# Attention, gated and bilinear layers on one core: query scaling moved to GpSimd, conversion passes and loads moved in time

## The chip, the cores and the metric

The kernel runs on one core of one Trainium2 chip. The metric is the device time of one execution in microseconds; the median of three runs of the kernel before is 1085.52 us (1084.79 to 1085.8). All rows below come from one profiled execution of that kernel.

## The reference

Three layers follow one another. All inputs but q, k, v and tau come as float64.

```python
scores = (1/8) * q @ k.T                 # 4 batches, 8 heads, 576 tokens, head size 64
thresh = max(scores) - tau               # scores below it are dropped
attn   = exp(scores - max(scores)) over the kept ones, divided by its sum
x = (attn @ v)                           # laid out as 2304 tokens x 512
h = x @ w_in;  y = (h * tanh(softplus(h))) @ w_out        # 512 -> 2048 -> 512
out = ((y @ w_a) * (y @ w_b)) @ w_out2                    # 512 -> 1536 -> 512
```

## The kernel before, in words

The first quarter of the time is attention, the rest the two dense layers; the change touches attention alone. The core works on 16 pairs of heads (4 batches, 4 pairs each). A pair is five units: c = 0 to 3 are 128 query rows each for both heads, c = 4 holds the last 64 rows of both heads at once. That makes 80 units, n = 0 to 79, and the loop in `attention` (L833) has one iteration per unit, written out by hand: the order of the calls is the order on each engine, and each engine works through its own list in order.

In iteration n these happen:

- `least` (L683), VectorE: reads the scores of unit n from PSUM, multiplies them by the constant column `nsc` (minus 1/8), writes them as `s` to SBUF and accumulates their least value `m`. One instruction per head.
- `bars` (L692), GpSimd: one small addition, `te` = `m` + tau.
- `turned` (L736): TensorE turns the masked weights of unit n-2, ScalarE copies them out of PSUM (`pt`).
- `expo` (L696), ScalarE: the exponential `ex` of unit n.
- `weighted` (L755), TensorE: products with v of unit n-4, into `sums_o`; ScalarE copies them out as `u`.
- `scores` (L669), TensorE: the scores of unit n+1. PSUM has room for one unit, so they need `least` of unit n to have read it.
- `mask` (L705), VectorE: reads `s` and `ex` from SBUF, writes `pm`. It belongs to unit n-1. After the last unit of a pair `invert` (L712) does two tiny VectorE operations on `sm`, and `send` (L787) multiplies `u` by the inverse sums and writes it to DRAM as `xd`.

Between them lies other work. The float64 weights are narrowed to float32 in `narrow` (L94), one block per pair of heads, 15 blocks during attention (`ask`, L796, starts one; `convert(n, k)`, L803, runs its next stage k units after the unit `due`, which has c = 4):

- k = 0: ScalarE takes the low words (L107, "low pass") and then the high words (L109, "sign-seeing pass")
- k = 1: VectorE shifts (L111), GpSimd adds (L112)
- k = 2: ScalarE takes the sign (L119)
- k = 3: GpSimd multiplies (L123, the "conversion product"), SyncE writes the block to DRAM

Inputs come through SyncE's queue. `load_qk` asks for q and k of the next pair at c = 0, `load_v` for v at c = 4. `prepare(0, 0)` (L255) sets up the first dense layer: four loads of `xd` into tiles `b` (first calls `b<-xd`), and for each a ScalarE pass `H` (L290, `x<-b`) and a VectorE pass `L` (L294, the remainder). Its plan at n = 48 puts the loads at n = 49, 59, 64, 54 and the passes H, L, H, L, ... at n = 52, 55, 57, 60, 62, 65, 67, 70.

Of the kernel before, what the change touches and what calls it, by code (L numbers as in the profile page):

```python
# [8 lines left out]
F32 = mybir.dt.float32  # L9
F32R = mybir.dt.float32r  # L10
I32 = mybir.dt.int32
I16 = mybir.dt.int16
U32 = mybir.dt.uint32
AF = mybir.ActivationFunctionType
ALU = mybir.AluOpType
PSUM = bass.MemoryType.PSUM
# [23 lines left out]
SEEN = 0.501 / (1.125 * 2.0 ** -15)  # L40
# [3 lines left out]
def tile_attn_mish_bilinear(ctx, tc, qd, kd, vd, vd2, tau, w_in, w_out, w_a, w_b, w_out2, out):  # L44
    nc = tc.nc
    V, A, G, PE = nc.vector, nc.scalar, nc.gpsimd, nc.tensor
# [11 lines left out]
    nsc = const.tile([128, 1], F32, name="nsc")  # L58
# [35 lines left out]
    def narrow(kind, f):  # L94

        w, block, _ = SOURCES[kind]
        shape, nm = [128, CC, 128], f"{kind}{f}"
        tl = lambda s, dt, bufs: cv.tile(shape, dt, tag="cv" + s, name=s + nm, bufs=bufs)
        raw = cv.tile([128, CC, 256], U32, tag="wraw", name="raw" + nm, bufs=3)
        nc.sync.dma_start(out=raw, in_=block(w, f).bitcast(U32))  # L100
        words = raw.rearrange("p c (n t) -> p t c n", t=2)
        hi, lo = words[:, 1], words[:, 0]
        for _ in range(WAIT[len(mish_on)]):
            yield True
        early = not mish_on
        a, o = tl("a", I32, 2), tl("f", F32, 2)
        A.activation(unit[:, 0::2].rearrange("p (c n) -> p c n", c=CC), lo, AF.Copy, scale=2.0 ** -29)  # L107
        if early:
            A.activation(o.bitcast(I32), hi.bitcast(F32), AF.Copy, scale=SEEN)  # L109
            yield True  # L110
        V.tensor_scalar(out=a, in0=hi.bitcast(I32), scalar1=3, scalar2=None, op0=ALU.logical_shift_left)  # L111
        (G if early else V).tensor_tensor(  # L112
            out=a, in0=a, in1=unit.bitcast(I32).rearrange("p (c n) -> p c n", c=CC), op=ALU.add
        )
        if not early:
            A.activation(o.bitcast(I32), hi.bitcast(F32), AF.Copy, scale=SEEN)
        yield True
        if early:
            A.activation(o, o.bitcast(I32), AF.Sign)  # L119
        else:  # L120
            V.tensor_scalar(out=o, in0=o.bitcast(I32), scalar1=-1.0, scalar2=1.0, op0=ALU.max, op1=ALU.min)
        yield True
        (G if early else V).tensor_tensor(out=o, in0=a.bitcast(F32), in1=o, op=ALU.mult)  # L123
        nc.sync.dma_start(out=wfd[kind][f // 2][:, f % 2], in_=o)
        written.add((kind, f))

    written = set()
    jobs = []
    if wide:
# [383 lines left out]
    for i, st in enumerate(steps):  # L513
        if st.same:
            continue
        for kind in st.kinds:
            if i:
                early = st.first and st.layer and kind == "a"
# [88 lines left out]
    with late_pools:  # L607
# [4 lines left out]
        qk = early_pools.enter_context(tc.tile_pool(name="qk", bufs=1))  # L612
        ps_s = early_pools.enter_context(tc.tile_pool(name="ps_s", bufs=1, space=PSUM))
        pairs = [(b, p) for b in range(B) for p in range(NP)]
# [3 lines left out]
        def load_qk(pi):  # L618

            b, p = pairs[pi]  # L620
            q = qk.tile([128, 640], F32, tag="qr", name=f"qr{pi}", bufs=2)
            k = qk.tile([128, S], F32, tag="k", name=f"k{pi}", bufs=3)
            first = 128 if pi == 0 else 640
            nc.sync.dma_start(out=q[:, :first], in_=qd[b, p][:, :first])
            (nc.scalar if pi == 0 else nc.sync).dma_start(out=k, in_=kd[b, p])
            if first < 640:
                nc.sync.dma_start(out=q[:, first:], in_=qd[b, p][:, first:])
            return dict(q=q, k=k)

        def load_v(pi):  # L630
            b, p = pairs[pi]
            v = at.tile([128, 9, 128], F32, tag="v", name=f"v{pi}", bufs=2)
            nc.sync.dma_start(out=v, in_=vd[b, p])
            both = at.tile([128, 5, 128], F32, tag="v2", name=f"v2{pi}", bufs=2)
            nc.sync.dma_start(out=both, in_=vd2[b, p])
            return v, both
# [3 lines left out]
        def warm(n):  # L640

            warmed.append(n)
            w = ps_t.tile([128, 4, 128], F32, tag=f"tp{len(warmed) % 2}", name=f"warm{len(warmed)}")
            for _ in range(n):
                PE.matmul(w[:, 0], ident, ident, start=True, stop=True)
# [23 lines left out]
        def scores(u, d):  # L669

            u["sp"] = [
                ps_s.tile([128, 2, 512], F32, tag="sp", name=f"sp{u['nm']}_{h}", bufs=2) for h in range(u["h"])
            ]
            for half in range(2):
                keys = slice(half * 288, half * 288 + 288)
                for h, sp in enumerate(u["sp"]):
                    if u["h"] == 2:
                        r, cols = HEADS[h], slice(u["c"] * 128, u["c"] * 128 + 128)
                        PE.matmul(sp[:, half, 0:288], d["q"][r, cols], d["k"][r, keys], start=True, stop=True)  # L679
                    else:  # L680
                        PE.matmul(sp[:, half, 0:288], d["q"][:, 512:640], d["k"][:, keys], start=True, stop=True)  # L681

        def least(u, h):  # L683

            if h == 0:
                u["s"] = at.tile([128, 2, S], F32, tag="s", name="s" + u["nm"], bufs=2)
            V.tensor_scalar(  # L687
                out=u["s"][:, h].rearrange("p (a c) -> p a c", a=2), in0=u["sp"][h][:, :, 0:288],
                scalar1=nsc, scalar2=None, op0=ALU.mult, op1=ALU.min, accum_out=u["m"][:, h:h + 1],
            )  # L690

        def bars(u):  # L692
            n = u["h"]
            G.tensor_tensor(out=u["te"][:, :n], in0=u["m"][:, :n], in1=bar2[:, :n], op=ALU.add)  # L694
# [6 lines left out]
        def COL(u, h):  # L701
            col = h * 4 + u["c"] if u["c"] < 4 else 8
            return slice(col, col + 1)

        def mask(u, h):  # L705
            V.scalar_tensor_tensor(  # L706
                out=u["pm"].rearrange("p a c -> p (a c)")[:, h * S:(h + 1) * S], in0=u["s"][:, h],
                scalar=u["te"][:, h:h + 1], in1=u["e"][:, h], op0=ALU.is_le, op1=ALU.mult,
                accum_out=u["pair"]["sm"][:, COL(u, h)],
            )  # L710

        def invert(pi):  # L712

            sm = pair[pi]["sm"]
            V.tensor_scalar(out=sm, in0=sm, scalar1=1e-9, scalar2=None, op0=ALU.add)
            pair[pi]["r"] = r = at.tile([128, 9], F32, tag="r", name=f"r{pi}", bufs=2)
            V.reciprocal(r, sm)
# [85 lines left out]
        def convert(n, k):  # L803

            for item in list(active):
                stages, due = item
                if n - due == k:
                    for _ in range(1 if k else 4):
                        if next(stages, None) is None:
                            active.remove(item)  # L810
                            break
# [5 lines left out]
        def plan(n, items):  # L817

            for at_, item in items:
                ahead.setdefault(n + at_, []).append(item)  # L820

        def attention():
            nonlocal mp, h_p, raw
            warm(8)
            data, vs = {0: load_qk(0)}, {}
            warm(6)
            data[1] = load_qk(1)
            vs[0] = load_v(0)
            us = {0: new_unit(0)}
# [3 lines left out]
            for n in range(len(units) + 5):  # L833
                u, prev, mid = us.get(n), us.get(n - 1), us.pop(n - 2, None)
                old = units[n - 4] if 4 <= n < len(units) + 4 else None
                convert(n, 1)
                convert(n, 3)
                if u:
                    pi, c = u["pi"], u["c"]
                    if c == 0 and pi:  # L840
                        if pi + 1 < len(pairs):
                            data[pi + 1] = load_qk(pi + 1)
                        data.pop(pi - 2, None)
                    if c == 4 and pi + 1 < len(pairs):
                        vs[pi + 1] = load_v(pi + 1)
                    for h in range(u["h"]):
                        least(u, h)
                    bars(u)
# [23 lines left out]
                ask(n)  # L872
                convert(n, 0)
                convert(n, 2)
                if prev:
                    for h in range(prev["h"]):
                        mask(prev, h)
                    if prev["c"] == 4:
                        invert(prev["pi"])
# [3 lines left out]
                    send(units[n - 10][0])  # L883
                if n == len(units) + 4:
                    send(len(pairs) - 2)
                if n == 48:
                    loads, rest = prepare(0, 0)
                    plan(0, zip((49, 59, 64, 54), loads))
                    plan(0, zip((52, 55, 57, 60, 62, 65, 67, 70), (item for _, item in rest)))
                if n == 66:  # L890
                    load, rest = first_weights(0)
                    load()
# [78 lines left out]
```

## Time and profile before

| | us |
|---|---|
| median of 3 runs | 1085.52 |
| lowest, highest | 1084.79, 1085.8 |
| the profiled execution, its time | 1084.55 |
| its span | 1082.8 |
| PE busy in the span | 1067.1 |
| VectorE (DVE) busy | 813.2 |
| ScalarE (ACT) busy | 628.5 |
| GpSimd (POOL) busy | 91.8 |

The span is the time from the first to the last instruction of the profiled execution. TensorE's busy time counts overlapping, pipelined matmuls and says little. A row of a timeline gives start, length, engine, source line, operation, result and operands, and in brackets the idle time of the engine ahead of it with what ended it. A row whose start is less than a length behind the one ahead of it overlaps it; the distance between two starts is the price of the first.

### The profile page before, as it was taken

How to read it: one execution, taken by the hardware profiler on the slowest of the kernel's cores; microseconds unless marked ns; L12 is line 12 of the kernel's file. 1: busy time of each engine (PE TensorE's matmuls, PEld its weight loads, DVE VectorE, ACT ScalarE, POOL GpSimd, SP SyncE). 2: the span in 40 equal slices, each digit the busy share in tenths (PEclk: the TensorE clock that was granted, in tenths of full speed). 3: DMA queues.
4: the chain of work that ended last, by engine and by line, in shares of the span. 5: the costliest groups of instructions: out<-in, count | busy, mean ns of one | idle time of the engine just before them, and what ended most of it. 6: DMA issues, size and time to landing. Idle time of an engine off the chain costs nothing.

```text
span 1082.8 us, 19717 instructions
## 1 busy us (share of the span) xinstructions
PE 1067.1 (99%) x7434; PEld 938.3 (87%) x7434; DVE 813.2 (75%) x1753; ACT 628.5 (58%) x1236; POOL 91.8 (8%) x117
## 2 busy tenths in 40 slices
PE   9999999999999999999999999999999999999998
PEld 6666666666899999999999999999999999999997
DVE  6999998989477787788667897777766656666653
ACT  5899988888576567556665574443343323433321
POOL 2333333332000000000000000000000000000000
PEclk9999999999999999999999999999999999999999
DMA  5366557564679749694599865436214442143401
GB/s 196 118 204 202 167 180 215 156 218 136 191 247 316 248 177 334 253 334 168 189 346 319 302 253 178 153 146 243 97 59 160 167 179 88 50 156 122 168 13 59
DMA packets 77711, 203.21 MB, mean 188 GB/s; under 512 B 6832, under 2 KB 36272, under 8 KB 73776
## 3 DMA queue, kind: packets, MB, share of 16 engines
q1 hardware_dynamic: 73152, 172.29, 47.0%
q10 hardware_dynamic: 4464, 29.66, 6.8%
q8 instruction: 58, 0.95, 0.3%
q14 instruction: 37, 0.30, 0.1%
HBM read 146.01 MB, written 55.91 MB: 186 GB/s over the span
## 4 chain that ended last, share of the span: by engine, by line
PE 86%; ACT 5%; DMA 4%; DVE 3%; issue 2%; SPq 1%; ACTq 0%; POOL 0%; DVEq 0%; POOLq 0%
PE acc L462 32%; PE sums_o L769 4%; PE sp L679 4%; PE tp L742 3%; ACT ex L699 2%; DMA b<-xd 2%; ACT pt L743 1%; PE sp L681 1%; DVE pm L706 1%; DVE s L687 1%; DMA inv<-rd 1%; PE sums_o L773 1%; PE h2i L342 1%; PE h5i L342 1%; PE h7i L342 1%
## 5 line engine op out<-in xcount | busy, mean ns | idle before, releaser
L462 PE MATMUL acc<-g,woo 128*128 128x256 f32 (+1 forms) x1152 | 225.4, 338 | 0.0
L462 PEld LDWEIGHTS acc<-g,woo 128*128 128x128 f32 x1152 | 181.3, 189 | 16.6
L462 PE MATMUL acc<-g,wop 128*128 128x512 f32 (+1 forms) x864 | 170.8, 338 | 0.0
L462 PEld LDWEIGHTS acc<-g,wop 128*128 128x128 f32 x864 | 137.4, 188 | 13.4 <-DVE g L391 0.9
L687 DVE TENSOR_SCALAR_CACHE_REDUCE s<-sp,nsc 128x576 f32<-128x576 f32 x144 | 112.5, 815 | 19.6 <-PE sp L679 14.1
L699 ACT ACTIVATE ex<-s,m 128x576 f32<-128x576 f32 x144 | 111.0, 772 | 11.8 <-DVE s L687 10.8
L706 DVE SCALAR_TENSOR_TENSOR pm<-s,te,ex 128x576 f32<-128x576 f32 x128 | 99.7, 815 | 1.1 <-ACT ex L699 1.1
L769 PE MATMUL sums_o<-pt,v 128*64 128x256 f32 x640 | 83.7, 391 | 5.3 <-ACT u L779 3.9
L743 ACT ACTIVATE pt<-tp 128x512 f32<-128x512 f32 x128 | 75.2, 588 | 22.3 <-PE tp L742 21.0
L679 PE MATMUL sp<-k,qr 64*128 64x288 f32 x512 | 86.5, 434 | 0.0
L385 DVE TENSOR_TENSOR g<-hs,g 128x384 fp32r<-128x384 f32 x96 | 51.8, 554 | 35.1 <-ACT g L384 34.9
L679 PEld LDWEIGHTS sp<-k,qr 64*128 64x128 f32 x512 | 51.2, 188 | 29.7 <-issue 15.4
L694 POOL TENSOR_TENSOR te<-m,bar 128x2 f32<-128x2 f32 (+1 forms) x80 | 52.8, 660 | 129.7 <-DVE s L687 102.5
L769 PEld LDWEIGHTS sums_o<-pt,v 128*64 128x64 f32 x640 | 40.4, 137 | 26.6 <-ACT u L779 5.9
L742 PEld LDWEIGHTS tp<-ident,pm 64*128 64x128 f32 x1024 | 45.8, 139 | 19.0 <-ACT pt L743 6.1
L742 PE MATMUL tp<-ident,pm 64*128 64x64 f32 x1024 | 53.1, 227 | 4.0 <-ACT pt L743 3.4
L485 ACT ACTIVATE ys<-acc 128x512 f32<-128x512 f32 (+1 forms) x44 | 21.3, 488 | 29.6 <-PE acc L462 25.4
L390 ACT ACTIVATE g<-s 128x384 fp32r<-128x384 f32 x18 | 9.5, 526 | 40.2 <-DVE s L441 40.1
L390 ACT ACTIVATE g<-c22b 128x384 fp32r<-128x384 f32 x18 | 9.5, 526 | 37.3 <-DVE c22b L441 37.3
L178 DVE TENSOR_TENSOR woo<-wfo,woo 128x512 fp32r<-128x512 f32 x46 | 30.6, 684 | 0.0
L177 ACT ACTIVATE woo<-wfo 128x512 fp32r<-128x512 f32 x46 | 26.8, 628 | 3.0 <-PE acc L462 2.6
L290 ACT ACTIVATE x<-b 128x768 fp32r<-128x768 f32 x24 | 20.2, 843 | 11.1 <-DMA b<-xd 4.7
(643 smaller groups left out, 2155.7 us busy)
## 6 DMA issues: line engine op xcount, KB each, us to landing
wia<-wpa SPq DMA_DIRECT2D x10, 1792.0 KB
wpi<-wii ACTq DMA_DIRECT2D x7, 1792.0 KB
wii<-wpi SPq DMA_DIRECT2D x7, 1792.0 KB
wfo<-wfo SPq DMA_DIRECT2D x23, 512.0 KB
wpa<-wia ACTq DMA_DIRECT2D x6, 1792.0 KB
v<-vd SPq DMA_DIRECT2D x16, 576.0 KB
rawi<-w_in SPq DMA_DIRECT2D x16, 512.0 KB
rawo<-w_out SPq DMA_DIRECT2D x16, 512.0 KB
```

The costliest lines, as they stand in the source:

```text
L178: lambda: V.tensor_tensor(out=dst()[1], in0=src(), in1=f32(dst()[0]), op=ALU.subtract),
L342: PE.matmul(st.bank, w[:, a, 2 * i + j, c * 128:(c + 1) * 128], x[:, b, c], start=j == c == m == 0, stop=j == c == 1 and m == 2,)
L385: at_gap(gap + 1, lambda: V.tensor_tensor(out=gl, in0=hs, in1=f32(gh), op=ALU.subtract))
L462: PE.matmul(ps, w[:, a, f, c * 128:(c + 1) * 128], st.g[f][:, b, cols], start=st.first and f == 0 and m == 0 and (kind == "c" or c % 2 == ...
L679: PE.matmul(sp[:, half, 0:288], d["q"][r, cols], d["k"][r, keys], start=True, stop=True)
L687: V.tensor_scalar(out=u["s"][:, h].rearrange("p (a c) -> p a c", a=2), in0=u["sp"][h][:, :, 0:288], scalar1=nsc, scalar2=None, op0=ALU.mul ...
L694: G.tensor_tensor(out=u["te"][:, :n], in0=u["m"][:, :n], in1=bar2[:, :n], op=ALU.add)
L699: A.activation(u["e"][:, h], u["s"][:, h], AF.Exp, bias=u["m"][:, h:h + 1], scale=-1.0)
L706: V.scalar_tensor_tensor(out=u["pm"].rearrange("p a c -> p (a c)")[:, h * S:(h + 1) * S], in0=u["s"][:, h], scalar=u["te"][:, h:h + 1], in ...
L742: PE.transpose(tiles[h][:, j], u["pm"][r, j], ident[r, r])
L743: moves = [lambda h=h: A.activation(u["pt"][:, 0:n, HEADS[h]], tiles[h][:, 0:n], AF.Copy) for h in range(2)]
L769: PE.matmul(po[r], v[0][:, j + 4 * h, r], pair[pi][c & ~1][:, :, j + 4 * h], start=j == 0, stop=j == 4)
```

## The change

- `least` multiplies by the constant 1.0. The factor goes to the queries: a new tile `qs` (two buffers) holds q times `nsc`. For pair 0 ScalarE makes it in two pieces ahead of the loop, for each later pair GpSimd makes it in one instruction at c = 1 of the pair before. `scores` reads `qs`.
- `load_qk` is called at c = 3, two pairs ahead, instead of at c = 0, one pair ahead.
- In `narrow`, while attention runs: stage k = 0 holds the low pass alone, k = 1 shift and addition as before, k = 2 the sign-seeing pass, k = 5 the sign, k = 8 the conversion product. The product also waits for the last `mask` issued ahead of it.
- `prepare(0, 0)` is planned at n = 43: loads at n = 44, 50, 53, 47, passes at n = 52, 54, 57, 59, 62, 64, 67, 69.

```diff
+        def sign():
+            A.activation(o.bitcast(I32), hi.bitcast(F32), AF.Copy, scale=SEEN)
         A.activation(unit[:, 0::2]..., lo, AF.Copy, scale=2.0 ** -29)
         if early:
-            A.activation(o.bitcast(I32), hi.bitcast(F32), AF.Copy, scale=SEEN)
             yield True
         V.tensor_scalar(out=a, ...); (G if early else V).tensor_tensor(out=a, ...)
-        if not early:
-            A.activation(o.bitcast(I32), hi.bitcast(F32), AF.Copy, scale=SEEN)
+        if early:
+            yield True
+        sign()
         yield True
...
-        (G if early else V).tensor_tensor(out=o, in0=a.bitcast(F32), in1=o, op=ALU.mult)
+        it = (G if early else V).tensor_tensor(out=o, in0=a.bitcast(F32), in1=o, op=ALU.mult)
+        if early:
+            behind_masks(it)     # a wait on masked[0], the last mask issued so far
...
+            qs = qk.tile([128, 640], F32, tag="qs", name=f"qs{pi}", bufs=2)
+        def scale_q(d, cols):
+            A.activation(d["qs"][:, cols], d["q"][:, cols], AF.Copy, scale=nsc)
...
-                scalar1=nsc, scalar2=None, op0=ALU.mult, op1=ALU.min, accum_out=...
+                scalar1=1.0, scalar2=None, op0=ALU.mult, op1=ALU.min, accum_out=...
...
             data, vs = {0: load_qk(0)}, {}
+            scale_q(data[0], slice(0, 128))
             warm(6)
+            scale_q(data[0], slice(128, 640))
...
                 convert(n, 1)
-                convert(n, 3)
+                convert(n, 8)
-                    if c == 0 and pi:
-                        if pi + 1 < len(pairs):
-                            data[pi + 1] = load_qk(pi + 1)
+                    if c == 3:
+                        if pi + 2 < len(pairs):
+                            data[pi + 2] = load_qk(pi + 2)
+                    if c == 1 and pi + 1 < len(pairs):
+                        d = data[pi + 1]
+                        G.tensor_scalar(out=d["qs"], in0=d["q"], scalar1=nsc, scalar2=None, op0=ALU.mult)
...
                 convert(n, 0)
                 convert(n, 2)
+                convert(n, 5)
...
-                if n == 48:
+                if n == 43:
                     loads, rest = prepare(0, 0)
-                    plan(0, zip((49, 59, 64, 54), loads))
-                    plan(0, zip((52, 55, 57, 60, 62, 65, 67, 70), (item for _, item in rest)))
+                    plan(0, zip((44, 50, 53, 47), loads))
+                    plan(0, zip((52, 54, 57, 59, 62, 64, 67, 69), (item for _, item in rest)))
```

## Rows read from the trace of the kernel before

**Rows 1.** Busy time of each engine in two stretches (--windows: stretch, length, PE, PEld, DVE...)
```profile
108.00:135.00 27.00, 26.71 (x315) 18.60 (x312) 25.98 (x69) 24.17 (x48) 10.47 (x12) 1.00 0.51 165
162.00:189.00 27.00, 24.91 (x252) 16.41 (x252) 23.06 (x62) 21.76 (x43) 8.41 (x10) 0.94 0.69 211
```

**Rows 2.** Timeline, VectorE, a regular pair (pair 6, c = 0 to 2)
```profile
100.92 0.76 DVE L791 TENSOR_TENSOR u<-u,inv 128x576 f32<-128x576 f32 x1
101.59 0.42 DVE L111 TENSOR_SCALAR ai<-rawi 128x512 int32<-128x512 int32 x1
101.93 0.82 DVE L687 TENSOR_SCALAR_CACHE_REDUCE s<-sp,nsc 128x576 f32<-128x576 f32 x1
...
103.41 0.81 DVE L706 SCALAR_TENSOR_TENSOR ph<-s,te,ex 128x576 f32<-128x576 f32 x1
...
104.26 0.17 DVE L715 TENSOR_SCALAR sm<-sm 128x9 f32<-128x9 f32 x1
...
104.78 0.82 DVE L687 TENSOR_SCALAR_CACHE_REDUCE s<-sp,nsc 128x576 f32<-128x576 f32 x1
...
108.09 0.82 DVE L687 TENSOR_SCALAR_CACHE_REDUCE s<-sp,nsc 128x576 f32<-128x576 f32 x1 [0.26 <-PE sp L679]
```

**Rows 3.** Timeline, first leasts of pairs 7, 10, 11, 12, 15; one pass L
```profile
117.65 0.82 DVE L687 TENSOR_SCALAR_CACHE_REDUCE s<-sp,nsc 128x576 f32<-128x576 f32 x1
...
164.82 0.81 DVE L687 TENSOR_SCALAR_CACHE_REDUCE s<-sp,nsc 128x576 f32<-128x576 f32 x1
...
183.91 0.82 DVE L687 TENSOR_SCALAR_CACHE_REDUCE s<-sp,nsc 128x576 f32<-128x576 f32 x1 [2.54 <-PE sp L679]
...
200.13 0.81 DVE L687 TENSOR_SCALAR_CACHE_REDUCE s<-sp,nsc 128x576 f32<-128x576 f32 x1
...
220.28 0.96 DVE L294 TENSOR_TENSOR x<-b,x 128x768 fp32r<-128x768 f32 x1
...
252.23 0.81 DVE L687 TENSOR_SCALAR_CACHE_REDUCE s<-sp,nsc 128x576 f32<-128x576 f32 x1
```

**Rows 4.** Timeline, ScalarE: the four passes H
```profile
175.95 0.85 ACT L290 ACTIVATE x<-b 128x768 fp32r<-128x768 f32 x1 [1.79 <-DMA b<-xd]
193.58 0.84 ACT L290 ACTIVATE x<-b 128x768 fp32r<-128x768 f32 x1
211.13 0.84 ACT L290 ACTIVATE x<-b 128x768 fp32r<-128x768 f32 x1 [1.22 <-DMA b<-xd]
229.09 0.84 ACT L290 ACTIVATE x<-b 128x768 fp32r<-128x768 f32 x1 [1.66 <-DMA b<-xd]
```

**Rows 5.** Chain of work that ended last, 172 to 190 us (start, length, what)
```profile
166.14 9.73 DMA b<-xd
```

**Rows 6.** Timeline, TensorE: first scores, and a product of unit c = 2
```profile
7.12 1.24 PE L679 MATMUL sp<-k,qr 64*128 64x288 f32 x8
...
105.37 1.52 PE L769 MATMUL sums_o<-pt,v 128*64 128x256 f32 x12 [0.28 <-ACT u L779]
```

**Rows 7.** Timeline, ScalarE: sign-seeing pass, sign, next instruction
```profile
101.41 0.69 ACT L109 ACTIVATE fi<-rawi 128x512 int32<-128x512 f32 x1
...
107.37 0.62 ACT L119 ACTIVATE fi<-fi 128x512 f32<-128x512 int32 x1
108.58 0.60 ACT L743 ACTIVATE pt<-tp 128x512 f32<-128x512 f32 x1 [0.59 <-PE tp L742]
```

**Rows 8.** Timeline, GpSimd: the first bar, then a regular pair
```profile
10.04 0.20 POOL L694 TENSOR_TENSOR te<-m,bar 128x2 f32<-128x2 f32 x1 [8.70 <-DVE s L687]
...
102.16 1.27 POOL L112 TENSOR_TENSOR ai<-ai,unit 128x512 int32<-128x512 int32 x1 [1.85 <-ACT fi L109]
103.63 0.64 POOL L694 TENSOR_TENSOR te<-m,bar 128x2 f32<-128x2 f32 x1 [0.20 <-DVE s L687]
...
108.12 1.27 POOL L123 TENSOR_TENSOR fi<-ai,fi 128x512 f32<-128x512 f32 x1 [0.98 <-POOL te L694]
```

**Rows 9.** Timeline, SyncE's queue: the inverse sums' writes of a pair
```profile
113.87 0.60 SPq L729 DMA_DIRECT2D rd<-rt  x2
```

More of the change, by code (lines that the diff above doesn't have):

```diff
@@ L122, in narrow, with behind_masks @@
         yield True
-        (G if early else V).tensor_tensor(out=o, in0=a.bitcast(F32), in1=o, op=ALU.mult)
+        it = (G if early else V).tensor_tensor(out=o, in0=a.bitcast(F32), in1=o, op=ALU.mult)
+        if early:
+            behind_masks(it)
         nc.sync.dma_start(out=wfd[kind][f // 2][:, f % 2], in_=o)
         written.add((kind, f))
+    masked = [None]
+    def behind_masks(it):
+        tc.add_manual_dep(it.ins, masked[0].ins.name, in_turn, reason="beside passes that read PSUM")
+    in_turn = mybir.DependencyInfo(mybir.DependencyClass.Sync, mybir.DependencyReason.DATA)
     written = set()
@@ L627, in load_qk @@
                 nc.sync.dma_start(out=q[:, first:], in_=qd[b, p][:, first:])
-            return dict(q=q, k=k)
+            return dict(q=q, k=k, qs=qs)
+        def scale_q(d, cols):
+            A.activation(d["qs"][:, cols], d["q"][:, cols], AF.Copy, scale=nsc)
         def load_v(pi):
@@ L678, in scores @@
                         r, cols = HEADS[h], slice(u["c"] * 128, u["c"] * 128 + 128)
-                        PE.matmul(sp[:, half, 0:288], d["q"][r, cols], d["k"][r, keys], start=True, stop=True)
+                        PE.matmul(sp[:, half, 0:288], d["qs"][r, cols], d["k"][r, keys], start=True, stop=True)
                     else:
-                        PE.matmul(sp[:, half, 0:288], d["q"][:, 512:640], d["k"][:, keys], start=True, stop=True)
+                        PE.matmul(sp[:, half, 0:288], d["qs"][:, 512:640], d["k"][:, keys], start=True, stop=True)
         def least(u, h):
@@ L688, in least @@
                 out=u["s"][:, h].rearrange("p (a c) -> p a c", a=2), in0=u["sp"][h][:, :, 0:288],
-                scalar1=nsc, scalar2=None, op0=ALU.mult, op1=ALU.min, accum_out=u["m"][:, h:h + 1],
+                scalar1=1.0, scalar2=None, op0=ALU.mult, op1=ALU.min, accum_out=u["m"][:, h:h + 1],
             )
@@ L705, in mask @@
         def mask(u, h):
-            V.scalar_tensor_tensor(
+            masked[0] = V.scalar_tensor_tensor(
                 out=u["pm"].rearrange("p a c -> p (a c)")[:, h * S:(h + 1) * S], in0=u["s"][:, h],
@@ L836, in attention @@
                 convert(n, 1)
-                convert(n, 3)
+                convert(n, 8)
                 if u:
                     pi, c = u["pi"], u["c"]
-                    if c == 0 and pi:
-                        if pi + 1 < len(pairs):
-                            data[pi + 1] = load_qk(pi + 1)
-                        data.pop(pi - 2, None)
+                    if c == 3:
+                        if pi + 2 < len(pairs):
+                            data[pi + 2] = load_qk(pi + 2)
+                        data.pop(pi - 1, None)
                     if c == 4 and pi + 1 < len(pairs):
                         vs[pi + 1] = load_v(pi + 1)
+                    if c == 1 and pi + 1 < len(pairs):
+                        d = data[pi + 1]
+                        G.tensor_scalar(out=d["qs"], in0=d["q"], scalar1=nsc, scalar2=None, op0=ALU.mult)
                     for h in range(u["h"]):
```

## The prediction

> **What bounds the kernel now.** I read first the busy time by stretches, then the timelines of one regular pair engine by engine, then the same for the pairs that last longer, and last the chain of waits there. In a regular stretch of attention three engines are nearly full at once: VectorE 25.98 and ScalarE 24.17 of 27 us, TensorE 26.71 [rows 1]. The change leaves the dense layers alone, so their time counts as unchanged.
>
> A regular pair takes 117.65 - 101.93 = 15.72 us [rows 2, 3]. VectorE sets it for most units: two leasts take 103.41 - 101.93 = 1.48, 0.74 each; the two leasts and two masks of c = 1 take 108.09 - 0.26 - 104.78 = 3.05, so a mask costs 0.74, too, and the last readout 0.09 [rows 2]. Going from c = 0 to c = 1 takes 2.85, from c = 1 to c = 2 takes 3.31, and only there a wait for scores stands in the row, 0.26. That wait hangs on TensorE, which itself waits 0.28 for a copy `u` of ScalarE [rows 2, 6].
>
> Pairs 10 to 14 are not regular. Their five first leasts to the next run from 164.82 to 252.23, 87.41 us [rows 3]; five regular pairs would take 78.6. So 8.8 us are lost there. The reader sees why in the passes H: three of four find ScalarE idle for their tile `b`, 1.79, 1.22 and 1.66, together 4.67 us [rows 4]. The loads are asked three units ahead, some 9.5 us, and the chain has 9.73 us for the first to land [rows 5]. ScalarE works in order, so exponentials and copies stand behind H; the next pair's first least then waits 2.54 us for scores [rows 3]. In that stretch the granted clock has a mean of 0.94 of full speed, so a part of it ran at 1.2 and not at 2.4 GHz; TensorE had gaps there, 24.91 busy of 27 [rows 1].
>
> **The change part by part.**
>
> *Loads of `b` earlier.* They are asked 8, 10, 12 and 14 units ahead of their H instead of three. Eight units are 25 us (at 15.72 / 5), against 9.73 to land [rows 3, 5], so all three waits go. They need `xd` of pairs that were sent off at n = 49 at the latest, ahead of n = 53; at n = 53 they stand ahead of v in SyncE's queue, which is used five units later. What H itself costs shows in pair 11, whose H found its tile there (193.58, no idle shown): 200.13 - 183.91 = 16.22, 0.50 above regular, and this pair also held a pass L [rows 3, 4]. So H costs nothing and L about 0.5 each. Pair 14 also holds passes of the first weights, which stay; for them I leave 0.4, an estimate, half the length of an H [rows 4]. Waits, therefore: 8.8 - 4 x 0.5 - 0.4 = 6.4 us. Bounds: 4.67 (ScalarE's idle alone) to 8.8.
>
> *Passes L move* from c = 0 to c = 4. One L takes 0.96 less the overlap of `send` with the next (0.76 long, 0.67 from start to start), so 0.87 [rows 2, 3]. Before, it came behind c = 0's leasts and a part of it lay in the 0.26 wait for scores. At c = 4 it delays the leasts of c = 0, hence its exponentials, the copy `u` behind them, the product that already waits for that copy, and the scores of c = 2 [rows 2, 6]: nothing on that way is slack, so I charge 0.85 in place of 0.5: 4 x 0.35 = 1.4 us lost. Bounds: 0 to 1.5.
>
> *Queries scaled on GpSimd.* 15 instructions. No row shows this operation there; the nearest are the conversion's, 512 elements with two inputs in 1.27, and the first bar, 2 elements, in 0.20 [rows 8]. So for 640 elements it lies between 0.20 and 0.20 + 640/510 x 1.07 = 1.54 us. I take 1.2, near the upper row since that has the size. GpSimd is idle there: behind `te` of c = 0 (ends 104.27) the next bar can't come before c = 1's leasts end, 104.78 + 2 x 0.74 = 106.26 [rows 2, 8]. But SBUF is not free to both engines. Alone, `te` takes 0.20; issued beside a mask it takes 0.64 and ends 0.05 after the mask (103.63 + 0.64 = 104.27, mask 103.41 + 0.81 = 104.22) [rows 2, 8]: it stands until the mask has read. So the scaling may run while VectorE reads PSUM (the leasts from 104.78 to 106.26), and ends by 105.8 even at 1.54. Queued behind it is the bar of c = 1, whose mask is a unit away. Cost 0, if VectorE's tiny addition of `invert` at 104.26 goes ahead of it; if not, see the slower rival. `qs` is ready three units before its scores. The new wait is for q to land, with the bar of c = 1 behind it; q is asked at c = 3 of the pair before, three units ahead, and in an emptier queue than the 9.73 of [rows 5], so I take 0.
>
> *1.0 in place of a column in `least`.* From 0 to what a least costs above its elements: `send` costs 0.67 per 576 elements (100.92 to 101.59), a least 0.74 [rows 2]. Two things can make that 0.07, the column and the readout of the accumulator, and a mask has both, too, so no row tells them apart. The readout is an instruction of its own, with 0.09 left behind the last mask, and explains all of it; I take 0; the other end is 144 x 0.07 = 10 us, of which at most some 9 would reach the end.
>
> *Conversion.* ScalarE's passes swap units: c = 4 has low pass and sign in place of low pass and sign-seeing pass (0.62 for 0.69), c = 1 the reverse, and ScalarE idles 0.59 behind its pass there [rows 7]. Sum 0, bounds -0.07 to +0.07 a pair, -1 to +1 in all. The product starts at the end of the last mask plus the 0.13 from VectorE to GpSimd (`te` starts at 103.63, the second least ends at 101.93 + 2 x 0.74 + 0.09 = 103.50) rather than at 108.12 [rows 2, 8]: masks of c = 0 end at 108.09 - 0.26 = 107.83, so at about 107.96, and 1.27 later, at 109.23, still ahead of the next mask at 109.57 (108.09 + 2 x 0.74) [rows 2, 8]. The bar of c = 2 stands behind it, as before. SyncE's write of the block follows it, as before. Cost 0; were it to run into a mask, that mask would be at most 1.27 late, but the new wait prevents it.
>
> *q and k at c = 3.* Two DMA issues per pair move in SyncE's queue from behind the inverse sums' writes, v, the load of the inverse and `xd` to ahead of them. SyncE is idle before those writes, which wait for ScalarE until 113.87, while the block's write at c = 2 is done soon after 109.39 [rows 8, 9]: two issues fit into four microseconds. Behind them v and the block of weights come no later. Nothing waited for q or k in the regular pair, so the gain is 0, too; a loss would need the 4 us gap to be filled, and v is used five units after its request.
>
> *The start.* ScalarE's two scalings lie before the first scores at 7.12, which follow the warming products without a gap [rows 6]; at the price of the nearest pass, 0.69 [rows 7], the loss is 0 to 0.7. I take 0.
>
> Sum: -6.4 + 1.4 = -5.0 us. The profiled execution, 1084.55, would become 1079.55; its span is 1082.8, the 1.75 around it stay. It lies 0.97 below the median, so for a median I say **1080.5**.
>
> **The rivals.**
>
> *GpSimd's scaling locks out VectorE (slower).* `te` ends at 104.27, and VectorE's addition in `invert` starts at 104.26 [rows 2, 8]: a hundredth of a microsecond decides which of two instructions on SBUF comes first. If the scaling wins and the addition has to wait for all of it, VectorE loses 0.2 to 1.5 us in 14 pairs, less the 0.26 wait at c = 1 that covers it. At 1.2 this is 14 x 0.94 = 13 us, 1093.5; at 1.54, 18 us, 1098.5. Slower overall from a wait of 5.0 / 14 + 0.26 = 0.62 up. For it: only GpSimd has been seen standing, never VectorE, but no long GpSimd operation stood there. Against it: the addition's start is a fixed step behind the mask, the scaling has first to be begun behind `te`. The Trainium skill, SBUF — State Buffer, section "Who interferes with whom", makes the case: whichever of the two starts first keeps the shared pair for its whole instruction, and a VectorE `tensor_scalar` from SBUF to SBUF can want that pair too. No row here shows VectorE losing. By GPSIMD Engine Reference, section "Engine selection", one-input work runs at about line rate; an estimate by that page is 0.75 us, and the rival would then be about 2 us slower than before.
>
> *The column was dear (faster still).* If all of the 0.07 of a least is its column, up to 9 us more go: 1071.5. Against it: the readout, which stays, would then cost nothing, though 0.09 of it shows behind the last mask [rows 2].
>
> *The waits go and little comes of it.* Only ScalarE's idle is regained, 4.67, and moved passes and the start take back 1.5 + 0.7 + 1: 1.5 us gained, 1084.0. For it: three engines are nearly full, so each delay finds a next holder. Against it: pair 11 shows what is left without the wait.
>
> **How the numbers follow.** Forecast (1078 to 1083) 0.60; locked out 0.20 (of which 0.06 end within 0.2% of before, at a short scaling); dear column 0.08; little regained 0.12 (half within 0.2%, half a little faster). A difference of 0.2%, 2.2 us, is about what a measurement of this kernel tells from none. Faster 0.60 + 0.08 + 0.06 = 0.74, same 0.06 + 0.06 = 0.12, slower 0.14. The range for 8 in 10 runs from 1076 to 1087; it leaves out most of the lock-out and the dear column.
>
> **What would show it.** The profile after should have no idle ahead of the four `x<-b`; pairs 10 to 14 at 15.7 to 16.6 each; regular pairs at 15.72; the scaling at about 104.3 in a pair like this, 0.7 to 1.6 long; `invert` still 0.04 behind its mask; products ending ahead of masks. It is wrong if regular pairs lengthen (lock-out: `invert` late by the length of the scaling), if they shorten (a least under 0.74), or if ScalarE finds `b` late again.

## The result, and the profile after

The changed kernel takes 1074.61 us (median of 5 runs, 1074.52 to 1075.43) against 1085.8 us before in the same comparison: ratio 0.9901, interval 0.9886 to 0.9915. That is 11.2 us faster, where 5.0 were forecast; it lies below the range given. The profiled execution of after took 1074.59 us with a span of 1072.8, 10.0 less than before. (Runs below were made in several groups; each is compared with the kernel before in its own group, whose median went from 1083.9 to 1084.7. Against those medians the gain would be 9.3 to 10.1 us, as the spans have it, so the 11.2 hold about 1 us of scatter.)

The forecast part came true. The stretch of pairs 10 to 14, busy time by engine as in [rows 1]; and the four passes H on ScalarE, which answer to [rows 4]:

```profile
162.00:189.00 27.00, 26.31 (x308) 18.48 (x304) 25.17 (x69) 24.63 (x49) 14.03 (x14) 1.00 0.72 223
```
```profile
171.43 0.85 ACT L303 ACTIVATE x<-b 128x768 fp32r<-128x768 f32 x1
187.65 0.85 ACT L303 ACTIVATE x<-b 128x768 fp32r<-128x768 f32 x1
204.06 0.84 ACT L303 ACTIVATE x<-b 128x768 fp32r<-128x768 f32 x1
220.13 0.85 ACT L303 ACTIVATE x<-b 128x768 fp32r<-128x768 f32 x1
```

No H waits any more, TensorE has 26.31 us in place of 24.91, and the granted clock is 1.00 through the stretch where it was 0.94. The first leasts of pairs 10 and 15 are now at 162.15 and 242.95, 80.80 us apart, where [rows 3] had 87.41.

The part that was not forecast shows in a regular pair, where the prediction had named it as a sign of being wrong: pairs that shorten, a least under 0.74. VectorE, the same pair as in [rows 2]; bracket: idle before, and what ended it:

```profile
100.06 0.76 DVE L704 TENSOR_SCALAR_CACHE_REDUCE s<-sp 128x576 f32<-128x576 f32 x1
100.74 0.10 DVE L704 DVE_READ_ACCUMULATOR s<-sp 128x1 f32 x1
100.74 0.76 DVE L704 TENSOR_SCALAR_CACHE_REDUCE s<-sp 128x576 f32<-128x576 f32 x1
...
101.42 0.82 DVE L723 SCALAR_TENSOR_TENSOR ph<-s,te,ex 128x576 f32<-128x576 f32 x1
...
102.28 0.19 DVE L732 TENSOR_SCALAR sm<-sm 128x9 f32<-128x9 f32 x1
...
103.10 0.76 DVE L704 TENSOR_SCALAR_CACHE_REDUCE s<-sp 128x576 f32<-128x576 f32 x1 [0.39 <-PE sp L696]
...
104.46 0.82 DVE L723 SCALAR_TENSOR_TENSOR pm<-s,te,ex 128x576 f32<-128x576 f32 x1
...
106.27 0.76 DVE L704 TENSOR_SCALAR_CACHE_REDUCE s<-sp 128x576 f32<-128x576 f32 x1 [0.25 <-PE sp L696]
...
115.54 0.75 DVE L704 TENSOR_SCALAR_CACHE_REDUCE s<-sp 128x576 f32<-128x576 f32 x1
```

A least has lost 0.06: it is 0.76 long where it was 0.82, as long as `send` with the same number of elements, and two take 101.42 - 100.06 = 1.36, 0.68 each, in place of 1.48. The readout of the accumulator is a row of its own and begins when the next instruction begins. The mask, with its column, keeps 0.82. The pair takes 115.54 - 100.06 = 15.48 us, 0.24 less. Nine leasts saved 0.54; a new wait of 0.39 for scores has come at c = 1.

GpSimd in that pair, against [rows 8]:

```profile
101.59 0.70 POOL L711 TENSOR_TENSOR te<-m,bar 128x2 f32<-128x2 f32 x1
102.27 1.88 POOL L867 TENSOR_SCALAR qs<-qr,nsc 128x640 f32<-128x640 f32 x1
104.70 0.64 POOL L711 TENSOR_TENSOR te<-m,bar 128x2 f32<-128x2 f32 x1 [0.55 <-DVE s L704]
106.11 1.29 POOL L127 TENSOR_TENSOR fi<-ai,fi 128x512 f32<-128x512 f32 x1 [0.77 <-DVE pm L723]
```

The scaling takes 1.88 us, beyond the bound of 1.54, and still ends at 104.15, 0.31 ahead of the next mask. It starts 0.01 ahead of VectorE's addition in `invert` (102.28), and that addition takes 0.19 in place of 0.17. The lock-out of the slower rival did not come.

Where 10.0 us of span went, from the first leasts of the pairs: the start 0.23 (first least of all at 8.16, before 8.39), pair 0 0.48, pairs 1 to 9 1.96 (141.46 to 139.50), pairs 10 to 14 6.61, all behind them 0.72 (of which 0.30 from the first to the last least of pair 15).

### The profile page after: what moved, and what is told of

Same layout as the page of the kernel before. It is cut to its first block, busy times and chain, and to the rows that moved or that the text cites. A ratio compares the mean times of both kernels' runs of the same rounds, so it can differ in the third digit from the quotient of the medians.

```text
span 1072.8 us, 19765 instructions
## 1 busy us (share of the span) xinstructions
PE 1060.9 (99%) x7434; PEld 934.3 (87%) x7434; DVE 804.0 (75%) x1753; ACT 629.5 (59%) x1238; POOL 118.1 (11%) x132
## 4 chain that ended last, share of the span: by engine, by line
PE 89%; ACT 5%; DVE 4%; issue 2%; DMA 0%; SPq 0%; ACTq 0%; POOL 0%; DVEq 0%; POOLq 0%
PE acc L475 33%; PE sums_o L786 5%; PE sp L696 4%; PE tp L759 3%; ACT ex L716 2%; DVE pm L723 2%; ACT pt L760 1%; DVE s L704 1%; PE sp L698 1%; PE h0i L355 1%; PE sums_o L790 1%; PE warm L662 1%; PE h4i L355 1%; PE h7i L355 1%; PE h6i L355 1%
## 5 line engine op out<-in xcount | busy, mean ns | idle before, releaser
L475 PEld LDWEIGHTS acc<-g,wop 128*128 128x128 f32 x864 | 137.4, 188 | 13.4 <-DVE g L404 0.8
L704 DVE TENSOR_SCALAR_CACHE_REDUCE s<-sp 128x576 f32<-128x576 f32 x144 | 103.8, 754 | 20.2 <-PE sp L696 16.3
L696 PE MATMUL sp<-k,qs 64*128 64x288 f32 x512 | 83.0, 428 | 0.0
L696 PEld LDWEIGHTS sp<-k,qs 64*128 64x128 f32 x512 | 49.0, 186 | 28.5 <-issue 11.9
L759 PE MATMUL tp<-ident,pm 64*128 64x64 f32 x1024 | 48.8, 226 | 1.0 <-ACT pt L760 0.7
L867 POOL TENSOR_SCALAR qs<-qr,nsc 128x640 f32<-128x640 f32 x15 | 28.2, 1880 | 0.0
```

Of the source, the lines that this page charges most:

```text
L475: PE.matmul(ps, w[:, a, f, c * 128:(c + 1) * 128], st.g[f][:, b, cols], start=st.first and f == 0 and m == 0 and (kind == "c" or c % 2 == ...
L696: PE.matmul(sp[:, half, 0:288], d["qs"][r, cols], d["k"][r, keys], start=True, stop=True)
L704: V.tensor_scalar(out=u["s"][:, h].rearrange("p (a c) -> p a c", a=2), in0=u["sp"][h][:, :, 0:288], scalar1=1.0, scalar2=None, op0=ALU.mul ...
L759: PE.transpose(tiles[h][:, j], u["pm"][r, j], ident[r, r])
```

## The experiments

Theory: two causes, loads asked early (about 5 us) and the constant in `least` (the rest). Rivals: all of it from the loads; a shorter least for another reason, the scaled queries or GpSimd's work beside it. The table gives for each kernel the median, its difference to the kernel before in its group, the mean length of a least, the length of a regular pair and the sum of pairs 10 to 14 (both from the starts of first leasts), all in us.

| kernel | median | to before | least | regular pair | pairs 10 to 14 |
|---|---|---|---|---|---|
| before | 1085.8 | | 0.814 | 15.72 | 87.41 |
| after | 1074.61 | -11.2 | 0.754 | 15.48 | 80.80 |
| e1, loads and passes alone | 1079.94 | -4.75 | 0.813 | 15.72 | 82.48 |
| e2, after without them | 1079.67 | -5.0 | 0.755 | 15.48 | 85.89 |
| e3, after with a column of ones | 1078.71 | -6.0 | 0.813 | 15.72 | 82.48 |
| e10, before with a constant | 1081.42 | -3.3 | 0.755 | 15.48 | 88.27 |
| e5, column at c = 1 to 3 | 1077.06 | -7.0 | 0.793 | 15.60 | 81.86 |
| e6, column at c = 4 and 0 | 1074.88 | -9.2 | 0.772 | 15.48 | 81.26 |
| e7, scaling twice | 1077.59 | -6.5 | 0.753 | 15.72 | 81.70 |
| e12, after, old passes | 1074.11 | -10.0 | 0.755 | 15.48 | 80.83 |
| e4, constant, no scaling | 1073.79 | -10.2 | 0.753 | 15.48 | 80.78 |
| e13, e4 with old passes | 1072.94 | -11.0 | 0.755 | 15.48 | 79.20 |
| e8, old conversion | 1074.59 | -9.4 | 0.753 | 15.48 | 80.76 |
| e11, no wait for a mask | 1074.52 | -9.9 | 0.754 | 15.48 | 80.77 |
| e14, less TensorE at c = 3 | 1072.87 | -11.1 | 0.753 | 15.38 | 80.68 |
| e15, less TensorE at c = 0 | 1073.88 | -10.6 | 0.753 | 15.48 | 80.78 |
| e16, copy of u first | 1070.72 | -13.4 | 0.753 | 15.35 | 78.99 |
| e18, a copy twice at c = 0 | 1080.71 | -3.4 | 0.753 | 15.89 | 82.85 |
| e17, best | 1069.58 | -14.5 | 0.754 | 15.35 | 78.44 |

**The two causes apart.** e1 gives the kernel before the new plan of loads and passes, e2 takes it out of the changed kernel.

```diff
-                if n == 48:
-                    plan(0, zip((49, 59, 64, 54), loads))
-                    plan(0, zip((52, 55, 57, 60, 62, 65, 67, 70), ...))
+                if n == 43:
+                    plan(0, zip((44, 50, 53, 47), loads))
+                    plan(0, zip((52, 54, 57, 59, 62, 64, 67, 69), ...))
```

> The kernel before with the four loads of b asked early and the passes at their new units, nothing else. Two-cause theory (early loads give 5 to 5.5 us, the constant in least gives the rest): 1080 to 1081 us, no idle ahead of the passes H, regular pairs stay at 15.72 us, a least stays at 0.815 us. Rival, all of the gain is of the loads: 1075 us. Rival, the loads only move their wait: over 1084 us.

> The changed kernel with loads of b and passes back at their old units. Two-cause theory: 1080 us, pairs 10 to 14 long again by some 5 us, regular pairs at 15.48 us. Rival, all of the gain is of the loads: 1085 us. Rival, q and k asked early are what let b land in time: 1075 us, b lands early enough at the old place, too.

e1: 4.75 us faster, pairs 10 to 14 4.93 shorter, regular pairs and leasts as before. e2: the four H wait again, 1.17, 0.87, 0.92 and 1.58 us, although q and k are asked early, and regular pairs stay at 15.48. So the loads are worth what was forecast and are no part of the rest.

e3 lets the least read a column of ones, e10 puts the constant -1/8 into the kernel before.

```diff
+    one = const.tile([128, 1], F32, name="one"); V.memset(one, 1.0)        # e3
-                scalar1=1.0, scalar2=None, op0=ALU.mult, op1=ALU.min, ...
+                scalar1=one, scalar2=None, op0=ALU.mult, op1=ALU.min, ...
```

> The changed kernel, but least multiplies by a column of ones in SBUF in place of the constant 1.0; GpSimd still scales the queries. Constant theory (reading the column costs a least 0.06 us): a least takes 0.815 us again, a regular pair 15.7 us, the time 1078 to 1079 us. Rival, the shorter least comes from scores of scaled queries, from the GpSimd work beside it or from another place: a least stays at 0.754 us and the time at 1074.6 us.

> The kernel before with the constant -1/8 in least in place of the column, nothing else: no scaling on GpSimd, old loads, old conversion. The factor's dependence on the sign of tau is left out. Constant theory: a least takes 0.754 us, a regular pair 15.5 us, the time 1081 to 1083 us. Rival, the constant matters only with scaling moved away: 1085.5 us. Ceiling, if VectorE alone set the pairs: 144 x 0.06 = 8.8 us less, 1077 us.

The least of e3, same columns as above; its own price returns with the column:

```profile
100.91 0.81 DVE L706 TENSOR_SCALAR_CACHE_REDUCE s<-sp,one 128x576 f32<-128x576 f32 x1
101.64 0.09 DVE L706 DVE_READ_ACCUMULATOR s<-sp,one 128x1 f32 x1
101.64 0.81 DVE L706 TENSOR_SCALAR_CACHE_REDUCE s<-sp,one 128x576 f32<-128x576 f32 x1
```

e3's pairs are those of e1 (15.72 and 82.48, pair 9 alone is longer, 16.01 against 15.71), though it scales on GpSimd and has the new conversion: in these pairs the column is the whole difference between e3 and after. e10 has the short least and the pair of 15.48 without any scaling. (Its pairs 10 to 14 are no shorter than before's; its four H waited 1.45 to 2.04.) Both rivals fall.

**GpSimd's scaling and the conversion.** e4 takes the scaling out and puts the factor into the constant; e8 brings the old stages back, without a wait for a mask; e11 leaves out the product's wait.

```diff
-                        G.tensor_scalar(out=d["qs"], in0=d["q"], scalar1=nsc, ...)      # e4
-                scalar1=1.0, ...
+                scalar1=-SCALE, ...
-            behind_masks(it)                                                            # e11
```

> The changed kernel with the constant -1/8 in least and no scaled queries: GpSimd's 15 scalings and ScalarE's two are gone. The factor's dependence on the sign of tau is left out. If the scaling is hidden beside the leasts, as the changed kernel's trace suggests: regular pairs 15.48 us, 1074.3 to 1074.9 us. Rival, its hold on SBUF costs VectorE something in each pair: 0.1 us or more less per pair, 1073 us or below.

> The changed kernel with the conversion's stages of before (both ScalarE passes of the high words early, product at k = 3) and no wait for a mask. If the spread of the passes and the wait are worth nothing: 1074.6 us, regular pairs 15.48 us. Rival, they are worth up to 1 us, the bound of the prediction: 1075.6 us, the product (1.28 us) runs into masks, masks longer than 0.815 us.

> The changed kernel without the product's wait for the last mask; the product then starts behind the bar of c = 1, in the middle of a mask. If a mask keeps GpSimd's two-input work standing and is not slowed itself: the product only looks longer (1.8 us), regular pairs 15.48 us, 1074.6 us. Rival, the product gets in between two masks and slows one of them by up to 0.4 us, as the second scaling did: regular pairs 15.6 to 15.9 us, 1076 to 1081 us.

Regular pairs are 15.48 in all three, the sums of pairs 10 to 14 agree to 0.04, and the times to 1 us. e4's median is 0.8 below after's, but from another group of runs, and only one of its pairs is clearly shorter: pair 9, 15.47 against 15.65 in after. e8 has 15.47 there, too, and e11 15.65; why was not tested. So in regular pairs the scaling is hidden, and the spread of the passes and the wait for a mask are worth nothing that the time shows. In e11 the product does meet a mask; GpSimd above, VectorE below:

```profile
105.60 1.87 POOL L127 TENSOR_TENSOR fi<-ai,fi 128x512 f32<-128x512 f32 x1
```
```profile
105.52 0.81 DVE L721 SCALAR_TENSOR_TENSOR pm<-s,te,ex 128x576 f32<-128x576 f32 x1
```

The product takes 1.87 in place of 1.27, the mask, begun 0.08 ahead of it, keeps 0.81: here GpSimd stands, and GpSimd has time. So it goes with the first 14 blocks. In the last block the product is 0.12 ahead, and it is VectorE that stands:

```profile
258.66 1.33 POOL L127 TENSOR_TENSOR fo<-ao,fo 128x512 f32<-128x512 f32 x1 [1.17 <-ACT fo L123]
```
```profile
258.78 1.83 DVE L721 SCALAR_TENSOR_TENSOR ph<-s,te,ex 128x576 f32<-128x576 f32 x1
```

That mask takes 1.83, where after, whose product waits, has 0.82: which of the two comes first decides who stands, and the product holds the mask nearly to its own end.

**What SBUF costs when GpSimd comes first.** e7 issues each scaling twice, so that the second meets masks; e12 puts L back behind c = 0, where it meets the scaling.

> The changed kernel with each of the 15 scalings on GpSimd issued twice, so that the second runs on into the masks of c = 0. Exclusive-lock theory (an instruction that holds the shared way into SBUF keeps it to its end): masks start 1 to 1.5 us late, regular pairs 16.4 to 17 us, 1088 to 1097 us. Rival, GpSimd yields to VectorE: masks keep their 0.815 us and their place, the second scaling takes longer than 1.88 us, 1074.6 to 1076 us.

> The changed kernel with loads of b early as they are, but the passes H and L at their old units (L at the end of c = 0, right behind the start of the scaling on GpSimd). Exclusive-lock theory: each L waits for the scaling to end, up to 1.5 us, pairs 11 to 14 take 17 us, 1077 to 1079 us. Rival, no lock between these two: L at c = 0 costs less than at c = 4 (0.5 in place of 0.76 us), 1073.5 us.

e7, GpSimd and VectorE, then e12, the same two:

```profile
105.62 1.89 POOL L868 TENSOR_SCALAR qs<-qr,nsc 128x640 f32<-128x640 f32 x1
107.47 0.35 POOL L711 TENSOR_TENSOR te<-m,bar 128x2 f32<-128x2 f32 x1
```
```profile
105.84 1.18 DVE L723 SCALAR_TENSOR_TENSOR pm<-s,te,ex 128x576 f32<-128x576 f32 x1
...
106.96 0.81 DVE L723 SCALAR_TENSOR_TENSOR pm<-s,te,ex 128x576 f32<-128x576 f32 x1
```
```profile
179.52 1.88 POOL L867 TENSOR_SCALAR qs<-qr,nsc 128x640 f32<-128x640 f32 x1
```
```profile
179.88 1.24 DVE L307 TENSOR_TENSOR x<-b,x 128x768 fp32r<-128x768 f32 x1
```

Neither theory held. The mask, begun 0.22 behind the scaling, loses 0.37 and is over at 107.02, while the scaling runs to 107.51; L, begun 0.36 behind, takes 1.24 in place of 0.95, 0.29 more. Both are held until about 0.6 us after the scaling began (0.22 + 0.37, 0.36 + 0.29), not to its end at 1.88. e7's pair grows by 0.24 of these 0.37. In six of e7's pairs the second scaling starts behind a mask and stands first; GpSimd, then VectorE:

```profile
185.07 2.25 POOL L868 TENSOR_SCALAR qs<-qr,nsc 128x640 f32<-128x640 f32 x1
```
```profile
184.76 0.81 DVE L723 SCALAR_TENSOR_TENSOR pm<-s,te,ex 128x576 f32<-128x576 f32 x1
...
185.50 1.35 DVE L723 SCALAR_TENSOR_TENSOR pm<-s,te,ex 128x576 f32<-128x576 f32 x1
```

The scaling is 0.37 longer, so it got going at about 185.44; the mask behind it loses 0.54 and got going at about 186.04, again 0.60 later. What the scaling does after these 0.6 us without holding VectorE these runs don't tell. An estimate from these rows: 0.6 us for 640 elements read and about 1.1 us for the product's 2 x 512 are both some 1 ns per element, as if GpSimd held VectorE while it reads its inputs; two shapes don't show it.

e13 takes both lessons: no scaling, so L at c = 0 meets nothing.

> The same with the passes H and L back at their old units, loads of b early. Without a scaling beside it, L at c = 0 should take 0.95 us again (1.24 beside the scaling) and cost some 0.5 in place of 0.76 us in each of four pairs: pairs 10 to 14 sum to 79.8 us against 80.8, 1073.2 to 1074 us. Rival, TensorE is the bound there whatever L does: 1074.5 us.

Pairs 10 to 14 sum to 79.20, 1.6 less than after.

**Where the other half of the leasts' saving stays.** 144 x 0.06 is 8.6 us, of which pairs 0 to 15 show 4.4. e5 and e6 give the column back to some of the leasts.

```diff
-                scalar1=1.0, ...
+                scalar1=one if 1 <= u["c"] <= 3 else 1.0, ...      # e5
+                scalar1=1.0 if 1 <= u["c"] <= 3 else one, ...      # e6
```

> The changed kernel with the column of ones read by the six leasts of c = 1 to 3 of each pair, the constant for the three of c = 4 and c = 0. If VectorE alone sets a pair: 6 x 0.06 = 0.36 us more per pair, 15.84 us, 1080 us. If TensorE has become the bound around c = 0 (its wait there is 0.39 us), TensorE catches up while VectorE is slow and the wait at c = 0 shrinks: a regular pair 15.5 to 15.7 us, 1076 to 1078 us.

> The changed kernel with the column of ones read by the three leasts of c = 4 and c = 0 of each pair, the constant for the others. If VectorE alone sets a pair: 0.18 us more per pair, 15.66 us, 1077.5 us. If TensorE is the bound around c = 0, the slower leasts fill its wait: a regular pair 15.48 to 15.55 us, 1074.6 to 1075.5 us.

e6: 15.48, so the constant is worth nothing at c = 4 and c = 0 once c = 1 to 3 have it. e5: 15.60, half of the way back to e3's 15.72. The first guess was a run of TensorE work as the bound there. e14 leaves out 16 of 20 instructions of the products of c = 4, e15 half of the products in iteration c = 0.

```diff
-            blocks = (range(3), range(3, 5))[c & 1] if c < 4 else range(5)
+            blocks = (range(3), range(3, 5))[c & 1] if c < 4 else range(1)                                      # e14
+            blocks = ((range(3), range(3, 5))[c & 1] if c != 1 else range(4, 5)) if c < 4 else range(5)      # e15
```

> The changed kernel without 16 of the 20 TensorE instructions of each unit c = 4 with v (0.76 of 0.95 us per pair), so that part of the attention output is wrong. If TensorE bounds a regular pair of the changed kernel: 15.0 to 15.2 us, the wait at c = 0 goes, 1067 to 1070 us. If VectorE bounds it: 15.4 to 15.48 us, 1073.5 to 1074.6 us.

> The changed kernel without half of the products with v that TensorE does in iteration c = 0 (one block of two of the unit before's second part, 0.5 us per pair), so that part of the attention output is wrong. They lie in the run from the transposes of c = 4 to the scores of c = 1, which has no gap. If that run bounds a regular pair: the 0.39 us wait of least at c = 1 shrinks to some 0.1, a pair takes 15.15 to 15.25 us, 1070 to 1071 us. Rival, the wait is for the product that waits for the copy u, or VectorE bounds the pair: 15.4 to 15.48 us, 1073.5 to 1074.6 us.

As the only bound it fell. e14's pair shrinks by 0.10 only, for 0.76 us of work; TensorE's transposes behind the missing products now wait for a mask:

```profile
111.05 0.46 PE L759 MATMUL tp<-ident,pm 64*128 64x64 f32 x8 [0.18 <-DVE pm L723]
```

In e15 the wait at c = 1 is gone (c = 0 to c = 1 takes 2.60 in place of 3.04), but TensorE then waits for ScalarE's copy of u, and the pair is 15.48 as before:

```profile
102.95 1.52 PE L786 MATMUL sums_o<-pt,v 128*64 128x256 f32 x12 [0.46 <-ACT u L796]
```

The chain of waits of after says a part of what holds a regular pair, from TensorE's transposes of c = 0 on (start, length, what):

```profile
100.02 0.53 PE tp L759 x16
100.55 0.33 ACT pt L760
100.88 0.15 issue
101.04 0.53 ACT ex L716
101.57 0.14 issue
101.70 0.59 ACT pt L760
102.29 0.27 ACT pt L766
102.57 0.66 ACT ex L716
103.23 0.28 ACT u L796
103.51 0.04 issue
103.56 1.51 PE sums_o L786 x12
```

Six ScalarE operations, then TensorE again until the next such transposes at 115.50, 15.48 later. The chain names no VectorE, but neither does that of the kernel before, whose pair the leasts did shorten: a wait inside a group of transposes is hidden in it. Further on in the chain of after, and VectorE's second mask of c = 2 with its readout:

```profile
108.97 0.28 PE tp L759 x7
109.25 0.01 issue
109.25 0.46 PE tp L759 x7
```
```profile
108.37 0.82 DVE L723 SCALAR_TENSOR_TENSOR pm<-s,te,ex 128x576 f32<-128x576 f32 x1
109.11 0.09 DVE L723 DVE_READ_ACCUMULATOR pm<-s,te,ex 128x1 f32 x1
```

The first eight of the 16 transposes start at most 0.06 apart, the ninth 0.23 behind the eighth, at 109.25: the second half needs this mask, whose readout ends at 109.20. In the kernel before the same group goes on at 111.18, 0.05 behind a readout, too. So a pair is a loop over three engines, and it adds up in both kernels:

| stretch | before | after |
|---|---|---|
| ScalarE at c = 0, to TensorE's product behind the copy of u | 102.23 to 105.37, 3.14 | 100.54 to 103.56, 3.02 |
| TensorE's product and scores, to the first least of c = 2 | 2.72 | 2.71 |
| VectorE's leasts and masks of c = 2, to the second half of the transposes | 108.09 to 111.18, 3.09 | 106.27 to 109.25, 2.98 |
| TensorE, to the next ScalarE run | 6.78 | 6.77 |
| sum | 15.73 | 15.48 |

The two leasts of c = 2 are in it, about 0.12 of the gain. The other 0.12 is a wait that the kernel before had in its ScalarE run: the exponential of c = 0 started 0.62 behind the copy ahead of it, 0.09 after the readout of its least had ended; in after it starts 0.50 behind the copy and 0.20 after the readout. Before, ScalarE and the readout on VectorE:

```profile
102.23 0.60 ACT L743 ACTIVATE pt<-tp 128x512 f32<-128x512 f32 x1
102.85 0.78 ACT L699 ACTIVATE ex<-s,m 128x576 f32<-128x576 f32 x1
```
```profile
102.67 0.09 DVE L687 DVE_READ_ACCUMULATOR s<-sp,nsc 128x1 f32 x1
```

e5 fits: its column at c = 2 costs 0.12. e6 fits: its columns at c = 4 and c = 0 lie outside these stretches. e16 moves the copy of u ahead of the second exponential, e18 makes the ScalarE run longer.

```diff
+                if back:
+                    back()
                 if u and u["h"] == 2:
                     expo(u, 1)
-                if back:
-                    back()
```

> The changed kernel with ScalarE's copy of u out of PSUM issued ahead of the second exponential of a unit instead of behind it. If ScalarE's run in c = 0 (copy, exponential, copy, copy, exponential, copy of u: 3.5 us) and TensorE's work behind it bound a regular pair: TensorE no longer waits for u at c = 1, VectorE becomes the bound at 15.35 to 15.4 us, 1073 to 1073.8 us. Rival, VectorE or TensorE alone bounds it, or the later exponential makes a mask late: 15.48 us or more, 1074.5 us or more.

> The changed kernel with one ScalarE copy (0.39 us, 0.27 from start to start) issued twice in each c = 0. If ScalarE's run in c = 0 lies in the loop that bounds a pair: the full 0.27 us per pair, 15.75 us, 1078.5 us. Rival, ScalarE has slack there: 15.48 us, 1074.5 us.

e16 has 15.35, TensorE's wait for u is gone, and c = 1 to c = 2 falls from 3.17 to 3.05, with no wait for scores left at c = 2. That is less than the copy's 0.27; VectorE, which no longer waits there, is the likely next bound, but this wasn't tested. With 13.4 us to before it gains more than was expected, since pairs 10 to 14 gain another 1.8. In e18 both copies took 0.69 from the first's start to the exponential behind them, 0.42 more, and a pair took 0.41 more:

```profile
104.30 0.80 ACT L766 ACTIVATE pt<-tc 128x256 f32<-128x256 f32 x2
104.99 0.77 ACT L716 ACTIVATE ex<-s,m 128x576 f32<-128x576 f32 x1
```

The 0.27 expected was too low (the second writes what the first writes; that this is why isn't shown), but the price is passed on in full. So ScalarE's run at c = 0 is part of the loop that bounds the pair of after, and of the 0.54 us that nine leasts saved only 0.24 lay on it. Everything favourable together, without scaling on GpSimd:

> All that the runs favour: loads of b early, passes at their old units, the constant -1/8 in least, no scaling on GpSimd, the copy of u ahead of the second exponential. The factor's dependence on the sign of tau is left out. If the copy's place gives 0.1 us per pair: 1071 to 1072 us. If it gives nothing: 1072.9 us.

1069.58 us, ratio 0.9867 (0.9853 to 0.9880) to before: better than both kernels. It keeps the constant -1/8 and so does not treat a negative tau as the others do.

## Why the prediction was wrong

*Loads of b and passes L.* Right, in mechanism and size. Forecast 5.0; e1 shortens pairs 10 to 14 by 4.93, and the time by 4.75. L at c = 4 was charged 0.85: e1's pairs 11 to 13 are 16.6, 0.88 above regular, and pair 14, for which 0.4 was left, is 16.10, 0.38 above; at c = 0 it was 0.50, and 15.82 - 15.48 = 0.34 in e13.

*1.0 in place of a column in `least`.* This is the step that failed. It was priced at 0, with 10 us as the other end and the rival "the column was dear" at a chance of 0.08. The column costs 0.06 us in each of 144 leasts, and 4.4 us reached the end: pair 0 0.48, pairs 1 to 9 1.96, pairs 10 to 14 82.48 - 80.80 = 1.68 (e1 to after), pair 15 0.30. The argument was that the accumulator's readout explains the 0.07 above `send`. It does not: after, a least with its readout takes 0.68 from start to start, `send` 0.67. The rows could have told. In [rows 2] a least is 0.82 long and `send` 0.76, and in the trace the readout is a row of its own that begins when the next instruction begins, so it can't be inside the 0.82. The second thing missed was the ceiling: "VectorE sets it for most units", and the rival's 9 us with it, took nearly all leasts as the bound, but the loop of a regular pair holds the two of c = 2 alone, and ScalarE's wait for one of c = 0. Loads and column make 4.93 + 4.42 of the 10.0 us of span; the start has 0.23, and for the 0.42 behind the leasts of pair 15 no run tells the cause.

*Queries scaled on GpSimd.* Hidden in regular pairs, as forecast, and for the reason given, but its length, 1.88, lay outside 0.20 to 1.54: a two-input row of other work was no upper end for a one-input operation with a column. The hole up to the next mask was long enough; it need not have been, since in e7 a mask begun 1.34 behind a scaling (106.96 to 105.62) kept its 0.81.

*The slower rival.* Its race was lost, as feared (102.27 against 102.28), but the price was wrong: 0.02 in each of 14 pairs and not the whole length. The rule of the Trainium skill, SBUF — State Buffer, section "Who interferes with whom", that whichever instruction starts first keeps the way to SBUF to its end, agrees with masks over GpSimd (`te` 0.20 to 0.64, the product 1.27 to 1.87) and nearly with the product over a mask (0.82 to 1.83 in e11), and not with the scaling over VectorE: e7's mask was done 0.49 ahead of the scaling's end.

*Conversion, q and k, start.* Priced at 0. For the conversion e8 agrees, but for 0.18 in pair 9. q and k were not undone alone. The start gained 0.23, but first leasts came anywhere from 7.3 to 8.8 in these runs, so nothing follows from it.

## What to carry to other kernels

Compare the length of an instruction with a neighbour's of the same element count before you call an operand free, and don't book a difference on a companion row that runs beside the next instruction. Before you multiply a saving by its count, look for the loop that the engine shares, and see that its stretches add up to the period: here two of a pair's nine leasts lay on it, and moving one ScalarE copy ahead was worth 3.9 us, nearly as much as the loads. Don't take a chain of waits for the loop where it merges instructions: a wait can lie inside a group. A transfer that makes an in-order engine wait costs all that stands behind it, and its price can be read pair by pair.

## What the hardware showed that was not expected

- A column as scalar operand costs `least`, a VectorE multiplication with an accumulated least over 576 elements from PSUM, 0.06 us over a constant (mean of 144: 0.813 in e3, 0.754 in after).
- On GpSimd a one-input multiplication by a column takes 1.88 us for 640 elements, more per element than the two-input product, 1.27 for 512.
- That multiplication holds VectorE's operations with two SBUF inputs for its first 0.6 us only (a mask 0.81 to 1.18, a pass L 0.95 to 1.24), whereas the two-input product holds a mask nearly to its own end (0.82 to 1.83), and a mask begun first makes GpSimd stand (the product 1.27 to 1.87).
